# Moving 144 products of the first pass behind attention, spacing the conversions anew, and adding the second pass's results by transfer

## The chip, the cores and the metric

The kernel runs on one core of a Trainium2 chip. The metric is the device time of one execution in microseconds, the median of several runs. TensorE (PE in the profile), VectorE (DVE), ScalarE (ACT), GpSimd (POOL) and SyncE (SP) each work through a queue of their own; SP's and POOL's queues also start transfers. TensorE's clock has two levels, 1.2 and 2.4 GHz, and the profile gives the granted clock as a share of the higher.

## The reference

Attention with a block-causal mask feeds a bilinear feed-forward network, all in float32:

```python
scores = scale * q @ k^T                    # 8 batches, 8 heads, 576 x 576, head size 64
scores = where(block_i >= block_j, scores, -1e9)      # blocks of 64
attn = exp(scores - max) / (sum + 1e-9)
x = (attn @ v) as (4608 tokens, 512)
out = ((x @ w_a) * (x @ w_b)) @ w_out       # 512 -> 1536 -> 512
```

## The kernel before

**Products.** Every float32 product is done as three TensorE products of rounded high and low parts (high by high, high by low, low by high). So each operand is split: ACT rounds the high part (L110), and DVE or POOL subtracts it to get the low part (L113).

**Three passes over the feed-forward network.** Its 1536 inner columns are 12 blocks of 128, and each pass does four of them for all tokens.

The *first pass* (`first_pass`, L545) runs inside attention. Attention is laid out in 66 slots, one for each of 64 heads and two more, each with a softmax, transposes (L468) and products with v of different heads, in an order given by the table `SLOT` (L595). Between these pieces the loop issues as many of the first pass's products as `want(now)` (L583 to L588) says are due: 36 a slot from slot 18 on, where `now` counts slots. A product is 288 columns wide (L217); `ab_unit` (L228) multiplies x by w_a and w_b, DVE forms `hf` from the two (L243), ACT and POOL split it into `hh` and `hl`, and `o_unit` (L248) multiplies by w_out. The result goes to a buffer in DRAM, `part[0]`. Of 2304 products, 288 are left when attention ends, and 48 more (`tail`) close the pass. The halves of x that the pass reads lie in `xpool`, three sets (L536).

The *second and third pass* run after attention, the loop over `ps_`, six tiles of 2 x 384 tokens each. `pair_unit` (L701) does 42 products for each block and two half-tiles at once, by sums of weights and of x; DVE combines the PSUM results into `u` (L729 to L736), which is split into `h_z` by ACT and POOL. `upool` has two buffers of `u`. Then `pair_out` (L743) does eight outputs of 12 products each (L757). For each output `load_part` (L809) has loaded the partial sum from DRAM by SP, `out` (L814) adds it on DVE and stores the sum by SP: the second pass reads `part[0]` and writes `part[1]`, the third reads `part[1]` and writes the result. `sums_x` (L669) prepares x for the next tile on DVE, ACT and POOL.

**Conversions of weights.** The weights come as 64-bit words and DVE turns them into float32 in several steps (`convert`, L127 to L150, `sums`, L161 to L178), 68 steps for four blocks. `background` issues steps beside TensorE's products by a pace: one step for each `STEP` = 800 ns of products in what is left of the first pass, for the second pass's weights; one for each `STEP2` = 2800 ns in tiles 1 to 5 of the second pass, for the third pass's, which are stored to DRAM and loaded again. What is still missing at the end of a stage comes at once (`background(1e4)`, L854).

The order of instructions on each engine is made by a scheduler from the order in which the code issues them; within an engine's queue an instruction that waits holds up all behind it.

Of the kernel before, what the change touches and what calls it, by code (L numbers as in the profile page):

```python
# [9 lines left out]
F32 = mybir.dt.float32  # L10
F32R = mybir.dt.float32r
# [3 lines left out]
ALU = mybir.AluOpType  # L15
AX = mybir.AxisListType

P = 128
# [12 lines left out]
PQ = lambda nc: nc.sync  # L31
# [6 lines left out]
XFB = 2  # L38
MORE = 6
PREF = True  # L40
STEP = 800
STEP2 = 2800
LATE = 1
LO2 = lambda nc: nc.vector
CONVP = [1]*12
# [7 lines left out]
def attention_then_bilinear_ffn(  # L53
# [10 lines left out]
    nc = tc.nc  # L64
    B, H, D, S = kT.shape
    SQ = qT.shape[3]
    NF = wab.shape[0]
    DO, T = outT.shape
# [3 lines left out]
    NPAIR = H // 2  # L72
# [4 lines left out]
    HT = S // 2  # L77
# [4 lines left out]

    dram = ctx.enter_context(tc.tile_pool(name="dram", bufs=1, space=bass.MemoryType.DRAM))
    xd = dram.tile([DO, T], F32, name="xd")
    part = [dram.tile([DO, T], F32, name=f"part{i}") for i in range(2)]
    wabd = dram.tile([F2, KP, P, 2 * NW * P], F32, name="wabd")
    wod = dram.tile([F2, P, 2 * DO], F32, name="wod")

# [170 lines left out]
    xpool = pool(left, "xpool", 2)  # L259
# [39 lines left out]
    if WARM:  # L299
        z = apool.tile([P, NCH, W], F32R, tag="al", name="z")[:, 0]  # L300
        nc.vector.memset(f32(z), 0.0)
        ps = ps_mm.tile([P, 512], F32, tag="mm", name="warm")
# [181 lines left out]
    def values(i):  # L484

        b, h = divmod(i, H)
        n = f"{b}_{h}"
        t = heads.pop(i)
        ah, al = t["a"]
        hp = h // 2  # L490
        if h % 2 == 0:
            xs_all.setdefault(b, {})[hp] = xpool.tile([P, S], F32, tag="xf", name=f"xf{b}_{hp}", bufs=XFB)
        xf = xs_all[b][hp]
        av = ps_t.tile([P, W], F32, tag="av", name=f"av{n}")
        xo = xf[(h % 2) * D:(h % 2 + 1) * D]
        if i < NATIVE:
            an, vr = ah, t["vr"]
            av0 = ps_t.tile([P, 512], F32, tag="tp", name=f"av0{n}", bufs=2)
            nc.tensor.matmul(av0[:D, :BLK], vr[:, NCH], an[:, SIDE, SC[0]], start=True, stop=True)
            nc.scalar.copy(xo[:, :BLK], av0[:D, :BLK])  # L500

            at = [0] + [P * c - BLK for c in range(1, NCH)] + [W - BLK, W]
            for g in range(NCH + 1):
                cols = slice(at[g], at[g + 1])
                last = min(g, NCH - 1)
                for c in range(last + 1):
                    mark = nc.tensor.matmul(
                        av[:D, cols], vr[:, c], an[:, c, cols], start=(c == 0), stop=(c == last and g < NCH)
                    )
                if g == 2:  # L510
                    yield mark
            nc.tensor.matmul(av[:D, W - BLK:], vr[:, NCH], an[:, SIDE, SC[1]], start=False, stop=True)
            nc.scalar.copy(xo[:, BLK:], av[:D])
        else:
            v2 = t["v2"]
            for c in range(NCH):
                mark = nc.tensor.matmul(av[:, c0[c]:], v2[:, c], ah[:, c, c0[c]:], start=(c == 0), stop=False)  # L517
            yield mark
            av0 = ps_t.tile([P, 512], F32, tag="tp", name=f"av0{n}", bufs=2)
            for j, a in enumerate((ah, al)):  # L520
                nc.tensor.matmul(av0[:, :P], v2[:, NCH], a[:, SIDE, SIDE_T * P:][:, :P], start=(j == 0), stop=(j == 1))
            for c in range(NCH - 1, -1, -1):
                mark = nc.tensor.matmul(av[:, c0[c]:], v2[:, c], al[:, c, c0[c]:], start=False, stop=(c == 0))  # L523

            lo = apool.tile([D, S + BLK], F32, tag="avlo", name=f"avlo{n}", bufs=1)
            lo0, lo = lo[:, :P], lo[:, P:]
            nc.scalar.copy(lo0, av0[D:, :P])
            nc.vector.tensor_tensor(xo[:, :BLK], av0[:D, :BLK], lo0[:, :BLK], op=ALU.add)
            nc.vector.tensor_tensor(lo0[:, BLK:], av0[:D, BLK:P], lo0[:, BLK:], op=ALU.add)
            nc.scalar.copy(lo, av[D:])  # L530
            nc.vector.tensor_tensor(lo[:, W - BLK:], lo[:, W - BLK:], lo0[:, BLK:], op=ALU.add)
            nc.vector.tensor_tensor(xo[:, BLK:], av[:D], lo, op=ALU.add)
        if h % 2 == 1:
            xs = []
            for j in range(2):
                xh, xl = (xpool.tile([P, HT], F32R, tag=f"x{z}", name=f"x{z}{b}_{hp}_{j}", bufs=3 * NPAIR) for z in "hl")  # L536
                split(xh, xl, xf[:, j * HT:(j + 1) * HT], nc.scalar, nc.gpsimd)
                xs.append((xh, xl))
            XQ(nc).dma_start(xd[hp * P:(hp + 1) * P, b * S:(b + 1) * S], xf)
            xs_all[b][hp] = xs  # L540
        yield mark
# [3 lines left out]
    def first_pass():  # L545
        late = None
        for b in range(B):
            for j in range(2):
                ts = slice(b * S + j * HT, b * S + (j + 1) * HT)
                hs = {}  # L550

                def out(o, ps, ts=ts):
                    ob = h_tile(1, HT, F32, f"ob{ts.start}_{o}")
                    nc.scalar.copy(ob, ps)
                    PQ(nc).dma_start(part[0][o * P:(o + 1) * P, ts], ob)

                for f in range(F1):
                    xs = [xs_all[b][hp][j] for hp in range(NPAIR)]
                    yield from ab_unit(f, xs, HT, f"{b}_{j}_{f}", hs)
                    if f == 0 and late:  # L560
                        yield from late
                late = o_units(range(F1), hs, HT, f"{b}_{j}", out)
        tail.append(late)
# [9 lines left out]
    NH = B * H  # L573
    LAG = 2
# [8 lines left out]
    def want(now):  # L583

        n = (now - H - LAG) * per_slot - behind
        if now < 2 * H + LAG:
            n = (H * per_slot - behind) * (now - MOE_FROM) / (2 * H + LAG - MOE_FROM)
        return int(n)  # L588

    keep = None  # L590

# [7 lines left out]
    for s in range(NH + LAG):  # L599
# [11 lines left out]
        for g, m in steps:  # L611
# [17 lines left out]
            now = s + due / fill  # L629
# [154 lines left out]
    for _ in moe:  # L784
        k += 1
        background(min(k * HT / 2.4 / STEP, F2 * PER_F))
    left.close()
# [8 lines left out]
    for _ in tail[0]:  # L796
        k += 1
        background(min(k * HT / 2.4 / STEP, F2 * PER_F))
    start, pace = k * HT / 2.4 / STEP, STEP
    k = 0  # L800


    for ps_ in range(2):
        fs = list(range(F1 + ps_ * F2, F1 + (ps_ + 1) * F2))
        for tt in range(NT2):
            lastp = ps_ == 1 and tt == NT2 - 1
            pt = {}

            def load_part(j, o):  # L809
                ts = slice((2 * tt + j) * T2, (2 * tt + j + 1) * T2)  # L810
                pt[j, o] = ppool.tile([P, T2], F32, tag="pt", name=f"pt{j}_{o}_{tt}_{ps_}"), ts
                nc.sync.dma_start(pt[j, o][0], part[ps_][o * P:(o + 1) * P, ts])

            def out(j, o, ps):  # L814
                t, ts = pt[j, o]
                nc.vector.tensor_tensor(t, ps, t, op=ALU.add)
                nc.sync.dma_start((part[1] if ps_ == 0 else outT)[o * P:(o + 1) * P, ts], t)
                i = todo.index((j, o)) + 6
                if i < len(todo):
                    load_part(*todo[i])  # L820
# [76 lines left out]
```

## Time and profile before

| | us |
|---|---|
| median of 3 runs | 1269.23 |
| lowest, highest | 1268.36, 1271.0 |
| the profiled execution | 1273.54 |
| its span in the trace | 1271.6 |

| engine | busy us | share of the span |
|---|---|---|
| PE | 1235.8 | 97% |
| DVE | 1006.1 | 79% |
| ACT | 683.3 | 54% |
| POOL | 556.9 | 44% |

The span is what the trace holds, the time of the execution is 1.9 us more. Attention with the slots takes the first 637 us or so; what is left of the first pass follows, then the second pass from 697 us and the third from 983 us. The shares are means over these stages, which differ: in most of them TensorE is busy all the time, and what matters is where it isn't, or where a stage takes longer than its products.

### The profile page before, as it was taken

Reading aid. Unit: us, or ns where it says so; the run is one execution under the profiler, and the core shown is the slowest. Engines: PE = TensorE matmul, PEld = TensorE weight load, DVE = VectorE, ACT = ScalarE, POOL = GpSimd, SP = SyncE. Lnnn points to the kernel's source line nnn. Section 1 sums busy time; section 2 is a strip of 40 time slices with the busy share of each in tenths; the row PEclk is TensorE's granted clock in tenths of the full one; section 3 lists DMA queues with packets and bytes.
Section 4 is the critical chain, followed back from the end, with each engine's and each line's share of the span. In section 5 each row is a group of like instructions: output and inputs, shape, how many; then the busy total and the mean of one; then the engine's idle time right before and its main releaser. Section 6 shows DMA issues by size and latency. Waiting matters only on the chain.

```text
span 1271.6 us, 23516 instructions
## 1 busy us (share of the span) xinstructions
PE 1235.8 (97%) x7849; PEld 1172.4 (92%) x7849; DVE 1006.1 (79%) x2389; ACT 683.3 (54%) x1722; POOL 556.9 (44%) x679
## 2 busy tenths in 40 slices
PE   9988999999999999999998999999999999999998
PEld 5668999999999999999998999999999899999998
DVE  6979877777887777877799999899879877577553
ACT  5788787878887788777745423323313322122210
POOL 4667566556565565665423223222222223123231
PEclk8999999999999999999998999999999899999999
DMA  5557767777667767676225264364287752243131
GB/s 197 147 162 198 193 166 182 184 169 180 173 164 185 170 175 174 164 179 162 88 95 161 96 195 132 109 195 155 86 286 260 240 149 83 67 149 103 48 100 62
DMA packets 93496, 196.58 MB, mean 155 GB/s; under 512 B 11968, under 2 KB 52928, under 8 KB 93376
## 3 DMA queue, kind: packets, MB, share of 16 engines
q1 hardware_dynamic: 88768, 185.64, 51.8%
q10 hardware_dynamic: 4608, 9.44, 2.0%
q8 instruction: 63, 1.03, 0.3%
q14 instruction: 57, 0.47, 0.1%
HBM read 96.47 MB, written 47.19 MB: 113 GB/s over the span
## 4 chain that ended last, share of the span: by engine, by line
PE 74%; DVE 14%; issue 3%; DMA 3%; ACT 3%; POOL 2%; SPq 0%; ACTq 0%; DVEq 0%; POOLq 0%
PE pso_z L757 14%; PE ps L217 12%; PE tp L468 7%; PE psx_z L711 7%; PE psw_z L711 6%; PE pso L217 5%; PE psv_z L711 5%; PE s L392 4%; PE av L517 3%; PE psy_z L711 3%; PE av L523 3%; PE sl L392 2%; DMA kp<-kT 2%; DVE sw L147 1%; DVE nm L398 1%
## 5 line engine op out<-in xcount | busy, mean ns | idle before, releaser
L113 POOL TENSOR_TENSOR h_z<-u_z,h_z 128x384 fp32r<-128x384 f32 x96 | 111.0, 1157 | 395.4 <-ACT h_z L110 370.2
L217 PE MATMUL ps<-xh,wab 128*128 128x288 f32 x1024 | 241.4, 303 | 1.2 <-ACT a L241 1.2
L445 POOL TENSOR_SCALAR e<-e,rc 128x512 f32<-128x512 f32 (+3 forms) x256 | 153.1, 610 | 125.3 <-DVE rc L442 118.6
L757 PE MATMUL pso_z<-h_z,wo 128*128 128x384 f32 x1152 | 203.4, 335 | 1.2 <-POOL h_z L113 1.2
L757 PEld LDWEIGHTS pso_z<-h_z,wo 128*128 128x128 f32 x1152 | 199.7, 188 | 2.6 <-POOL h_z L113 2.6
L217 PEld LDWEIGHTS ps<-xh,wab 128*128 128x128 f32 x1024 | 171.9, 188 | 4.7 <-ACT a L241 1.4
L472 DVE TENSOR_TENSOR al<-tp,ah 128x512 fp32r<-128x512 f32 x224 | 131.5, 608 | 34.0 <-ACT ah L470 33.8
L217 PE MATMUL ps<-xl,wab 128*128 128x288 f32 x512 | 153.9, 301 | 0.0
L468 PE MATMUL tp<-ident,e 128*128 128x128 f32 x832 | 135.8, 278 | 11.1 <-POOL e L445 4.0
L470 ACT CAST ah<-tp 128x512 fp32r<-128x512 f32 x224 | 116.6, 533 | 50.8 <-PE tp L468 47.9
L110 ACT CAST h_z<-u_z 128x384 fp32r<-128x384 f32 x96 | 49.4, 514 | 164.4 <-DVE u_z L736 157.3
L217 PE MATMUL pso<-hh,wo 128*128 128x288 f32 x512 | 128.1, 311 | 4.4 <-ACT hh L110 4.4
L468 PEld LDWEIGHTS tp<-ident,e 128*128 128x128 f32 x832 | 100.4, 141 | 26.8 <-POOL e L445 10.4
L711 PE MATMUL psx_z<-xh,wab 128*128 128x384 f32 x384 | 118.2, 344 | 4.3 <-DVE u_z L729 3.6
L401 ACT ACTIVATE e<-s,nm 128x192 f32<-128x192 f32 (+2 forms) x192 | 101.7, 530 | 32.0 <-DVE nm L398 23.0
L711 PE MATMUL psw_z<-xh,wab 128*128 128x384 f32 x384 | 117.1, 341 | 1.3 <-DVE u_z L731 1.3
L711 PE MATMUL psv_z<-xh,wab 128*128 128x384 f32 x384 | 117.0, 339 | 0.0
L398 DVE TENSOR_REDUCE nm<-s 128x1 f32<-128x192 f32 (+3 forms) x256 | 109.9, 431 | 2.4
L217 PEld LDWEIGHTS ps<-xl,wab 128*128 128x128 f32 x512 | 96.4, 188 | 3.4
L217 PEld LDWEIGHTS pso<-hh,wo 128*128 128x128 f32 x512 | 88.4, 192 | 6.6 <-ACT hh L110 5.3
L113 POOL TENSOR_TENSOR v<-vr,v 128x320 fp32r<-128x320 f32 x56 | 50.4, 899 | 87.8 <-ACT v L110 71.3
L392 PE MATMUL s<-k,q 128*128 128x256 f32 x336 | 81.3, 322 | 3.1 <-ACT e L401 1.5
(142 smaller groups left out, 2926.3 us busy)
## 6 DMA issues: line engine op xcount, KB each, us to landing
k<-kp SPq DMA_DIRECT2D x112, 288.0 KB, 3.6
xr<-xd SPq DMA_DIRECT2D x48, 384.0 KB, 3.4
pt<-part SPq DMA_DIRECT2D x96, 192.0 KB, 3.5
q<-qp SPq DMA_DIRECT2D x112, 160.0 KB, 2.6
raww<-wab SPq DMA_DIRECT2D x24, 512.0 KB, 3.8
qp<-qT SPq DMA_DIRECT2D x32, 320.0 KB, 3.2
vr<-vm SPq DMA_DIRECT2D x64, 160.0 KB, 3.2
kp<-kT SPq DMA_DIRECT2D x32, 288.0 KB, 3.5
```

What stands on the lines that cost most here:

```text
L110: nc.scalar.copy(hi, src)
L113: return lo_eng.tensor_tensor(lo, src, f32(hi), op=ALU.subtract)
L217: mm = nc.tensor.matmul(ps, w_, d_, start=(i == 0), stop=(i == n - 1))
L392: mark = nc.tensor.matmul(ps[:, :w], qm[:, q0[t]:q0[t] + P], kk[:, :w], start=(i == 0), stop=(i == len(ks) - 1))
L398: nc.vector.tensor_reduce(nm[:, t:t + 1], view, axis=AX.X, op=ALU.max, negate=True)
L401: nc.scalar.activation(out, view, AF.Exp, bias=bias, accum_out=sm[:, t, :1])
L445: nc.gpsimd.tensor_scalar(ev, ev, rc[:, t:t + 1], 1.0, op0=ALU.mult, op1=ALU.mult)
L468: mark = nc.tensor.transpose(tp[:, c], src, ident)
L470: nc.scalar.copy(ah[:, :m, cols], tp[:, :m])
L472: return nc.vector.tensor_tensor(al[:, :m, cols], tp[:, :m], f32(ah[:, :m, cols]), op=ALU.subtract)
L711: nc.tensor.matmul(ps, wt[:, i, iw], j[:, ix], start=start and kp == 0 and i == 0 and j is xh, stop=kp == KP - 1 and i == 1, skip_group_ch ...
L757: nc.tensor.matmul(ps, wt[:, a, osl], b, start=i == 0, stop=i == 3 * len(fs) - 1)
```

## The change

It has three parts.

1. `DEFER` = 144: `want` is lowered evenly over the 48 slots from 18 on, so that 33 products a slot are due there instead of 36, and 432 products (with the tail 480) are left when attention ends, not 288 (336). x keeps four sets in `xpool`, not three.
2. `STEP` goes from 800 to 1050 and `STEP2` from 2800 to 1900.
3. One `part` in DRAM. In the second pass `out` copies the PSUM result by ACT and starts a transfer from POOL's queue that adds it to `part` in DRAM (`accum_op`); the load of the partial sum, DVE's addition and SP's store are left out. The third pass is as before, but reads `part`.

```diff
-STEP = 800
-STEP2 = 2800
+DEFER = 144
+STEP = 1050
+STEP2 = 1900
...
-    part = [dram.tile([DO, T], F32, name=f"part{i}") for i in range(2)]
+    part = dram.tile([DO, T], F32, name="part")
...
-  xh, xl = (xpool.tile([P, HT], F32R, ..., bufs=3 * NPAIR) for z in "hl")
+  xh, xl = (xpool.tile([P, HT], F32R, ..., bufs=4 * NPAIR) for z in "hl")
...
-        return int(n)
+        return int(n - DEFER * max(now - 2 * H - LAG, 0) / (NH - 2 * H))
...
-                nc.sync.dma_start(pt[j, o][0], part[ps_][o * P:(o + 1) * P, ts])
+                if ps_ == 1:
+                    nc.sync.dma_start(pt[j, o][0], part[o * P:(o + 1) * P, ts])
...
-                nc.vector.tensor_tensor(t, ps, t, op=ALU.add)
-                nc.sync.dma_start((part[1] if ps_ == 0 else outT)[o * P:(o + 1) * P, ts], t)
+                if ps_ == 0:
+                    nc.scalar.copy(t, ps)
+                    nc.gpsimd.dma_start(part[o * P:(o + 1) * P, ts], t, accum_op=ALU.add)
+                else:
+                    nc.vector.tensor_tensor(t, ps, t, op=ALU.add)
+                    nc.sync.dma_start(outT[o * P:(o + 1) * P, ts], t)
...
-    nc = bacc.Bacc("TRN2", target_bir_lowering=False, num_devices=1)
+    nc = bacc.Bacc("TRN2", ..., num_devices=1, dynamic_dma_scratch_size=4096)
```

Line numbers of the changed kernel are one higher up to L586 and two higher behind it. Whole programs differ so: DVE 2376 rows and 2328, ACT 1436 and 1484, POOL 684 and 732 (48 of them transfers), SP 681 and 587; TensorE's number is the same.

Three places show what moves. The first is DVE's queue in what is left of the first pass, behind attention; rows with L139 to L178 (after: L140 to L179) are steps of the conversions, and `hf` is what TensorE's next products need. Before:

```order
L243 TENSOR_TENSOR hf_0_1_10093<-ps_7_0_1_10071,a_0_1_10069 128x288
L178 TENSOR_TENSOR wab_9847<-mw_0_10017,wab_9847 128x512
L147 SCALAR_TENSOR_TENSOR sw_1_10086<-raww_1_10014,sw_1_10086 128x512
L143 TENSOR_SCALAR mw_1_10087<-raww_1_10014 128x512
L145 SCALAR_TENSOR_TENSOR mw_1_10087<-raww_1_10014,mw_1_10087 128x512
L243 TENSOR_TENSOR hf_0_2_10137<-ps_7_0_2_10116,a_0_2_10114 128x288
L149 TENSOR_TENSOR xw_1_10088<-mw_1_10087,sw_1_10086 128x512
L172 TENSOR_TENSOR mw_1_10087<-xw_1_10088 128x128 x2
L172 TENSOR_TENSOR mw_1_10087<-mw_1_10087,xw_1_10088 128x128
L139 TENSOR_SCALAR sw_0_10165<-raww_0_10084 128x512
L172 TENSOR_TENSOR mw_1_10087<-xw_1_10088,mw_1_10087 128x128
L177 TENSOR_TENSOR wab_9847<-xw_1_10088,wab_9847 128x384
```

After, on the same queue:

```order
L244 TENSOR_TENSOR hf_1_2_9917<-ps_6_1_2_9897,a_1_2_9895 128x288
L140 TENSOR_SCALAR sw_1_9945<-raww_1_9849 128x512
L179 TENSOR_TENSOR wab_9649<-mw_0_9852,wab_9649 128x512
L144 TENSOR_SCALAR mw_1_9946<-raww_1_9849 128x512
L244 TENSOR_TENSOR hf_1_3_9961<-ps_6_1_3_9940,a_1_3_9938 128x288
L146 SCALAR_TENSOR_TENSOR mw_1_9946<-raww_1_9849,mw_1_9946 128x512
L148 SCALAR_TENSOR_TENSOR sw_1_9945<-raww_1_9849,sw_1_9945 128x512
L244 TENSOR_TENSOR hf_0_0_9997<-ps_7_0_0_9983,a_0_0_9981 128x288
```

Two or three steps stand between two `hf` where four to seven stood.

The second place is DVE's queue at the first unit of the third pass (`u_z_0_8`), whose four PSUM results TensorE can only go on with once `u` has read them. Before:

```order
L816 TENSOR_TENSOR pt_3_5_0_13308<-pso_3_z_5_13385,pt_3_5_0_13308 128x384
L143 TENSOR_SCALAR mw_2_13418<-raww_2_13400 128x512
L147 SCALAR_TENSOR_TENSOR sw_2_13417<-raww_2_13400,sw_2_13417 128x512
L145 SCALAR_TENSOR_TENSOR mw_2_13418<-raww_2_13400,mw_2_13418 128x512
L676 TENSOR_TENSOR xr_1_13531<-xr_1_13531 128x384
L149 TENSOR_TENSOR xw_2_13419<-mw_2_13418,sw_2_13417 128x512
L729 TENSOR_TENSOR u_z_0_8_13498<-psx_z_0_8_13467,u_z_0_8_13498 128x384
L139 TENSOR_SCALAR sw_2_13432<-raww_2_13415 128x512
L143 TENSOR_SCALAR mw_2_13433<-raww_2_13415 128x512
L731 TENSOR_TENSOR u_z_0_8_13499<-psw_z_0_8_13468,u_z_0_8_13498 128x384
```

After:

```order
L684 TENSOR_TENSOR xt_1_0_13633<-xr_1_13484,xt_1_0_13633 128x384
L677 TENSOR_TENSOR xt_1_1_13713<-xr_1_13488,xr_1_13486 128x384
L678 TENSOR_TENSOR xr_1_13486<-xr_1_13486 128x384
L681 TENSOR_TENSOR xt_1_1_13713<-xr_1_13488,xr_1_13486 128x384
L684 TENSOR_TENSOR xt_1_1_13713<-xr_1_13488,xt_1_1_13713 128x384
L731 TENSOR_TENSOR u_z_0_8_13449<-psx_z_0_8_13418,u_z_0_8_13449 128x384
L733 TENSOR_TENSOR u_z_0_8_13450<-psw_z_0_8_13419,u_z_0_8_13449 128x384
```

No conversion and no addition of `pt` stands there any longer; the rows ahead of `u` prepare x.

The third place is POOL's queue at the end of a tile of the second pass: `xl` is the next tile's x, `h_z_1_4` the split of the next tile's first unit. Before:

```order
L113 TENSOR_TENSOR h_z_0_7_0_10868<-u_z_0_7_10872,h_z_0_7_0_10867 128x384
L691 TENSOR_TENSOR xl_1_1_10919<-xr_1_10673,xh_1_1_10909 128x768
L692 TENSOR_TENSOR xl_1_1_10919<-xt_1_1_10910,xh_1_1_10909 128x384
L113 TENSOR_TENSOR h_z_1_4_1_11089<-u_z_1_4_11091,h_z_1_4_1_11088 128x384
L113 TENSOR_TENSOR h_z_1_4_0_11087<-u_z_1_4_11090,h_z_1_4_0_11086 128x384
```

After:

```order
L694 TENSOR_TENSOR xl_1_1_10912<-xt_1_1_10903,xh_1_1_10902 128x384
L821 DMA part<-pt_0_0_0_10751 128x384
L821 DMA part<-pt_1_0_0_10752 128x384
L821 DMA part<-pt_2_0_0_10753 128x384
L821 DMA part<-pt_3_0_0_10754 128x384
L821 DMA part<-pt_0_0_0_10755 128x384
L821 DMA part<-pt_1_0_0_10756 128x384
L821 DMA part<-pt_2_0_0_10942 128x384
L821 DMA part<-pt_3_0_0_10948 128x384
L114 TENSOR_TENSOR h_z_1_4_1_11081<-u_z_1_4_11083,h_z_1_4_1_11080 128x384
```

The tile's eight transfers stand between the two.

## Rows read from the trace of the kernel before

**Rows 1.** Windows by stage; the header names the columns, (x) counts instructions.

```profile
core 0: us, PE busy (x) PEld busy (x) DVE busy (x) ACT busy (x) POOL busy (x), PEclk, DMA share, GB/s
637.50:697.00 59.50, 52.37 (x366) 50.45 (x365) 57.64 (x114) 29.73 (x64) 15.06 (x13) 0.94 0.40 127
697.00:745.30 48.30, 47.32 (x266) 45.77 (x265) 47.89 (x81) 19.69 (x33) 15.58 (x12) 1.00 0.42 136
...
887.10:934.60 47.50, 47.16 (x266) 45.98 (x266) 40.57 (x65) 12.09 (x22) 13.26 (x10) 1.00 0.44 140
934.60:983.30 48.70, 47.09 (x265) 46.13 (x264) 40.13 (x66) 13.11 (x23) 13.24 (x10) 1.00 0.78 276
983.30:1035.80 52.50, 49.51 (x266) 48.71 (x265) 46.36 (x80) 19.03 (x31) 13.77 (x10) 0.93 0.67 219
1035.80:1082.30 46.50, 46.50 (x266) 46.33 (x266) 31.38 (x51) 11.38 (x20) 13.18 (x10) 1.00 0.35 104
```

**Rows 2.** Chain of waits in stage A: start, length, the work.

```profile
674.26 9.60 PE ps L217 x72
```

**Rows 3.** TensorE's waits, 637.5 to 746: total, times, longest, in us.

```profile
PE pso L217 <- ACT hh L110: 4.4, 4, 1.6
PE pso L217 <- POOL hl L113: 2.7, 4, 0.9
```

**Rows 4.** DVE's groups in stage A: count, busy us, mean ns, idle before.

```profile
L147 DVE SCALAR_TENSOR_TENSOR sw<-raww,sw 128x512 int32<-128x512 int32 x8 | 6.1, 763 | 0.0
...
L243 DVE TENSOR_TENSOR hf<-ps,a 128x288 f32<-128x288 f32 x10 | 4.5, 449 | 0.0
```

**Rows 5.** Windows of two stretches at a lower clock, columns as in Rows 1.

```profile
687.80:694.70 6.90, 4.81 (x19) 4.36 (x19) 6.87 (x14) 5.80 (x10) 1.66 (x2) 0.51 0.81 254
991.60:998.50 6.90, 6.12 (x19) 6.12 (x20) 6.31 (x13) 3.02 (x5) 0.34 (x1) 0.51 0.91 302
```

**Rows 6.** Timeline, third pass's start: start, length, engine, work, [idle before <-releaser].

```profile
989.82 0.44 PE L711 MATMUL psx_z<-xh,wab 128*128 128x384 f32 x1 [1.73 <-DVE u_z L729]
992.38 0.69 PE L711 MATMUL psw_z<-xh,wab 128*128 128x384 f32 x1 [1.25 <-DVE u_z L731]
...
989.21 0.55 DVE L729 TENSOR_TENSOR u_z<-psx_z,u_z 128x384 f32<-128x384 f32 x1
991.10 0.43 DVE L139 TENSOR_SCALAR sw<-raww 128x512 int32<-128x512 int32 x1 [1.34 <-DMA raww<-wo]
```

**Rows 7.** Windows of slots, L217 alone: length, PE, PEld, clock, DMA, GB/s.

```profile
135.47:174.53 39.06, 24.23 (x126) 18.93 (x124) 1.00 0.72 187
303.38:322.76 19.38, 13.28 (x74) 10.76 (x72) 1.00 0.76 194
175.00:626.00 451.00, 305.24 (x1656) 247.23 (x1656) 1.00 0.67 167
```

**Rows 8.** ACT's cast of `kp`, 175 to 626, and what ended its waits.

```profile
L344 ACT CAST kp<-kp x22: 672/674/696, 179.1 to 585.9; 128x576 fp32r<-128x576 f32 x22
...
  DMA q<-qp: 4.6, 3
  DMA kp<-kT: 1.3, 3
```

**Rows 9.** DVE's addition of `pt` in one tile, columns as in Rows 4.

```profile
L816 DVE TENSOR_TENSOR pt<-pso_z,pt 128x384 f32<-128x384 f32 x9 | 4.8, 547 | 0.0
```

**Rows 10.** Timelines of POOL, DVE and ACT around a tile's end.

```profile
779.43 2.58 POOL L691 TENSOR_TENSOR xl<-xr,xh 128x768 fp32r<-128x768 f32 x1
781.97 1.74 POOL L692 TENSOR_TENSOR xl<-xt,xh 128x384 fp32r<-128x384 f32 x1
...
800.83 1.03 POOL L113 TENSOR_TENSOR h_z<-u_z,h_z 128x384 fp32r<-128x384 f32 x1 [17.13 <-ACT h_z L110]
...
801.13 1.01 DVE L139 TENSOR_SCALAR sw<-raww 128x512 int32<-128x512 int32 x1
...
809.04 0.48 ACT L728 COPY u_z<-psy_z 128x384 f32<-128x384 f32 x1 [0.48 <-PE psy_z L711]
```

More of the change, by code (lines that the diff above doesn't have):

```diff
@@ L535, in values @@
             for j in range(2):
-                xh, xl = (xpool.tile([P, HT], F32R, tag=f"x{z}", name=f"x{z}{b}_{hp}_{j}", bufs=3 * NPAIR) for z in "hl")
+                xh, xl = (xpool.tile([P, HT], F32R, tag=f"x{z}", name=f"x{z}{b}_{hp}_{j}", bufs=4 * NPAIR) for z in "hl")
                 split(xh, xl, xf[:, j * HT:(j + 1) * HT], nc.scalar, nc.gpsimd)
@@ L554, in out @@
                     nc.scalar.copy(ob, ps)
-                    PQ(nc).dma_start(part[0][o * P:(o + 1) * P, ts], ob)
+                    PQ(nc).dma_start(part[o * P:(o + 1) * P, ts], ob)
                 for f in range(F1):
@@ L886 @@
     }
-    nc = bacc.Bacc("TRN2", target_bir_lowering=False, num_devices=1)
+    nc = bacc.Bacc("TRN2", target_bir_lowering=False, num_devices=1, dynamic_dma_scratch_size=4096)
     args = [
```

## The prediction

> **What bounds the kernel now.** I read the windows by stage first. TensorE is busy nearly everywhere, so the question is where a stage is longer than its products need. A product of 288 columns costs 9.60 us / 72 = 133 ns where nothing disturbs it [rows 2], and a tile of the second and third pass takes 46.5 us at its best, with PE busy for the whole of it [rows 1]. Against these two prices the stages after attention stand so. The stretch from 637.5 to 697.0, which I call stage A (the left-over products of the first pass), holds 366 products: 366 x 0.1333 = 48.8 us, but lasts 59.5, so 10.7 us over. The second pass's six tiles begin at 697.0; the first is 1.8 us over, the four from 745.3 to 934.6 together 189.3 - 186.0 = 3.3, the sixth 2.2. The third pass's first tile (983.3 to 1035.8) is 6.0 over [rows 1]. So two places are to be had: A and that last tile.
>
> In A the reader should look at DVE's column: 57.64 of 59.50 us busy [rows 1]. TensorE waits there for `hh` and `hl`, ACT's and POOL's halves of `hf`, 7.1 us up to 746 [rows 3]. `hf` is a short DVE operation (449 ns) that stands in a queue of conversions (763 ns for one of their kinds) [rows 4]. Behind the wait the clock falls: 0.51 granted, the 1.2 GHz level, for 6.9 us, and again for 6.9 us in the third pass's first tile [rows 5]. At half speed 6.9 us do the work of 3.5, so each costs about 3.4 us and is part of the 10.7 and the 6.0. The second place has the same cause: TensorE waits 1.73 and 1.25 us for `u_z`, two DVE operations of 0.55 us which run among conversions, one of which itself waited for its load [rows 6].
>
> In the slots TensorE is the bound too: 46 slots of 36 products take 451.0 us, 9.80 each, and an undisturbed pair 19.38, 9.69 each [rows 7].
>
> **The change, part by part.**
>
> *Fewer products in the slots.* 48 slots lose 3 products each: 144 x 0.1333 = 19.2 us, if TensorE stays the bound. It is uncertain that it does. The nearest rows are four early slots with about 31 products: 39.06 / 4 = 9.77 us, where a clean slot of 31 takes 9.69 - 5 x 0.1333 = 9.03. They lose 0.74 a slot, the slots of 36 only 9.80 - 9.69 = 0.11 [rows 7]. On a straight line, 33 products would lose 0.49, 0.38 more than now, 48 x 0.38 = 18 us, and the whole gain here would be gone. Against the line: those four still lie in the start-up, and slots of 36 are clean for dozens in a row. One thing does not shrink with PE's work: ACT's `kp` cast, once per two slots, waited for a load in 6 of 22 cases, 5.9 us [rows 8], and POOL and the pair's other work follow it. Every two slots become 0.8 us shorter (6 x 0.1333); if about half of that, 0.43, is lost in the six late pairs and in some eight others partly, that is some 4.3 us. With 0.7 for the edge from POOL's scaling to the transposes I take 5 us of give-back, nearer to the slots of 36 (33 is nearer to 36 than to 31); ends: -2 and +18. Term: -19.2 + 5 = -14.2.
>
> *The same products after attention, conversions further apart.* A then has 366 + 144 = 510 products, 68.0 us for TensorE. DVE's work there is its 57.64 plus six more `hf` (6 x 0.449 = 2.7): 60.3 us, now 8 under TensorE's where it was 9 over (57.6 against 48.8). So A turns from DVE-bound to PE-bound. What stays is that the last `hh` and `hl` have no products behind them to hide in: the longest waits, 1.6 + 0.9 [rows 3], and 0.5 elsewhere; 3 us over. The stretch at the lower clock goes with the long wait. A becomes 71 us: +11.5 against 59.5. Ends for what is left over: 0 and 7. The order shows conversions further apart between two `hf`, and the seven steps that no longer fit come with the first pair unit, where four PSUM banks of products stand ready; I take 0, with 1.5 either way.
>
> *Conversions of the third pass, faster.* 168 products of 160 ns in a tile are 26.9 us of the planner's time; at 2800 that is 9.6 steps, 48 in five tiles of the 68, and 20 come in one lump at the pass's end. At 1900 it is 14.1, 70.7 in five, so no lump is left. The first `u_z` of the third pass then find DVE free, as in the next tile (46.50 us) [rows 1]. I keep 0.4 over: -5.6. Ends: -6 and -2.
> The price lies in tiles 1 to 5 of the second pass: 4.5 more steps a tile at about 0.85 us is +3.9 of DVE, and the eight additions of `pt` go, 8 x 0.547 = 4.4 [rows 9]. DVE stays at about 40.6 of 47.5 [rows 1], so 0; ends -2 and +5.
>
> *Results added by the transfer.* In each tile of the second pass 8 loads on SP, 8 additions and 8 stores go; 8 ACT copies and 8 transfers issued by POOL come. ACT has the room: 12 of 47.5 us busy [rows 1], about 0.5 a copy [rows 10]. PSUM banks come free at the copy rather than at an addition that also waits for a load; no cost. POOL's issue is shown nowhere. Its place is: after `xl` (the last ends at 783.7, 8 us into a tile's output products), before the next tile's `h_z` (800.83) [rows 10]. `u` has two buffers, so the next tile's third unit needs the first unit's split to be over before its ACT copy at 809.04 [rows 10]. From 783.7 to there less two splits of 1.0 to 1.4 is 22 to 23 us, and TensorE has some 2 more before it misses `u`: 8 issues fit up to about 3.1 us each. Below that it costs nothing; above, 8 x (d - 3.1) a tile, six tiles. For d the nearest rows are POOL's own operations on a 128x384 tile, 1.03 to 1.74, and as a high bound its longest there, 2.58 [rows 10]. I take 1.2: 0 us. DRAM has room: 140 GB/s moved in such a tile, 276 where the weights load [rows 1].
> Here the slowest case hangs on DVE and POOL holding each other up: the conversion `L139` takes 1.01 us beside POOL's split and 0.43 alone [rows 6, 10]. The Trainium skill (page "SBUF — State Buffer", section "SBUF: two separate sides") says that GpSimd writes the descriptors of such transfers itself and is shut out while certain DVE operations run; a later section gives 620 ns alone and 3100 ns beside a DVE copy. The pair of 1.01 and 0.43 agrees that the two block each other; no run here shows it for transfers. By that figure eight issues would take 24.8 us, right at the limit, and the sum would hardly change.
>
> **The sum.** -14.2 (slots) + 11.5 (A) - 5.6 (third pass) = -8.3 us. The profiled execution took 1273.54, 4.3 above the median of 1269.23, which I take for something outside these terms; so 1265.2 for it and 1269.2 - 8.3 = 1261 for the median.
>
> **The rivals.** About 0.2% (2.5 us) is what a measurement of this kernel can tell from no change: faster is below 1266.7, slower above 1271.8.
> 1. *Slots at the early rate.* Attention's chain, not TensorE, sets the slot at 33 products. Price +18 in place of +5: 1261 + 13 = 1274, slower. It decides from 16 us of give-back (0.33 a slot). For it: the four slots of 31. Against: clean slots of 36, and the early place of the four. 0.13.
> 2. *DVE still binds A.* The conversions still stand ahead of `hf`, each later product waits as now, and A keeps its 10.7: 1261 + 7.7 = 1269, same. For it: still 60 of 71 us busy. Against: PE's queue has 144 products to take meanwhile. 0.12.
> 3. *POOL is held.* d = 4 gives 8 x 0.9 x 6 = 43 us: 1304, slower. Decides from d = 3.3, where 8 x 0.2 x 6 = 10 eats the gain. For it: DVE is 85% busy beside it. 0.06.
> 4. *The lump only spreads.* The 20 steps in the second pass's tiles make TensorE wait there, 5 us: 1266. 0.10.
> My forecast 0.59.
>
> **How the numbers follow.** Faster: 0.59 + 0.08 of rival 4 + 0.01 = 0.68. Same: rival 2 and the rest of 4, 0.14. Slower: rivals 1 and 3 with little less, 0.18. The forecast's own ends: best -2 slots, 0 over in A, -6: about 1251; worst with 10 of give-back and 5 in the tiles, 1271. The range 1252 to 1271 leaves out rivals 1 and 3 and a little below.
>
> **What would show it.** Right: slots about 9.5 us each on the mean (9.80 - 0.40 + 0.10); A about 71 us with DVE well under it; the third pass's first tile at 47 and full clock; POOL's `part` transfers over by the next tile's second unit; second-pass tiles at 47. Wrong: slots at 9.75 or more (rival 1); `hf` waits in A as long as before (2); `h_z` late for TensorE at a tile's second half (3); pass tiles at 48 (4). If A gains but the slots don't, the products were merely carried from one cover to no cover.

## The result and the profile after

The changed kernel takes 1274.67 us (median of 8 runs, 1274.07 to 1279.55), the kernel before 1270.12 in the same comparison (8 runs, 1263.68 to 1273.62): a ratio of 1.0042, 95% interval 1.0023 to 1.0061. It is 0.4% slower. The forecast was 1261 us, faster.

The two profiled executions, 1273.54 before and 1274.54 after, differ by 1.0 us only. That of before was 3.4 above its median, that of after at its median. Stage by stage (attention's end is the end of its last TensorE product; a tile runs from its first product to the next tile's):

| stage, us | before | after | difference | forecast |
|---|---|---|---|---|
| attention and slots, to the end of attention | 637.5 | 630.5 | -7.0 | -14.2 |
| rest of the first pass (A) | 59.5 | 68.4 | +8.9 | +11.5 |
| second pass, tile 0 | 48.3 | 48.9 | +0.6 | 0 |
| second pass, tiles 1 to 4 | 189.2 | 194.7 | +5.4 | 0 |
| second pass, tile 5 | 48.75 | 47.8 | -0.95 | 0 |
| third pass, tile 0 | 52.5 | 46.5 | -6.0 | -5.6 |
| the rest | 235.8 | 236.0 | +0.1 | 0 |

The windows of the changed kernel by stage answer to [rows 1], with the same columns: A, two tiles of the second pass, its last, the third pass's first.

```profile
core 0: us, PE busy (x) PEld busy (x) DVE busy (x) ACT busy (x) POOL busy (x), PEclk, DMA share, GB/s
630.50:698.90 68.40, 67.35 (x508) 67.02 (x507) 59.61 (x121) 35.69 (x77) 18.83 (x18) 1.00 0.33 105
747.70:796.30 48.60, 47.20 (x267) 45.79 (x266) 42.35 (x72) 20.15 (x38) 21.19 (x19) 1.00 0.50 128
796.30:845.10 48.80, 47.20 (x266) 45.88 (x265) 41.32 (x67) 19.89 (x38) 20.26 (x19) 1.00 0.54 145
942.40:990.20 47.80, 47.17 (x265) 45.91 (x265) 40.05 (x58) 18.64 (x34) 19.16 (x17) 1.00 0.81 244
990.20:1036.70 46.50, 46.50 (x266) 46.33 (x266) 31.61 (x51) 11.85 (x21) 15.33 (x13) 1.00 0.53 154
```

In A TensorE is busy 67.35 of 68.40 us, DVE 59.61, and the clock is at its full share, 1.00, where it was 0.94: the turn from DVE-bound to TensorE-bound came as forecast. The third pass's first tile is clean. The loss lies in two places: the slots, which give back more than forecast, and tiles 1 to 4 of the second pass, which should have cost nothing.

**The slots.** The 44 slots from 18 to 61 show it best. I take 9.69 us for a slot with 36 products, as in [rows 7], and three products less, 9.29, with 33; what the 44 slots take above that (426.4 and 408.8 us) I call the loss. It is 5.7 us before and 17.7 after. These are the windows of the 44 slots before and after, with L217 (after: L218) alone, and the columns length, PE, PEld, clock, DMA, GB/s:

```profile
174.50:606.60 432.10, 291.84 (x1586) 236.46 (x1584) 1.00 0.69 173
173.50:600.10 426.60, 276.87 (x1454) 220.15 (x1452) 1.00 0.68 173
```

Two slots alone, 24 and 36, last 13.4 and 13.2 us (9.9 and 9.8 before). What stands in slot 24, from the timelines of SP (issues), ACT, POOL and TensorE of the changed kernel:

```profile
223.83 0.60 SPq L359 DMA_DIRECT2D q<-qp  x1
...
227.89 0.34 SPq L323 DMA_DIRECT2D qp<-qT  x1
...
229.29 0.45 SPq L322 DMA_DIRECT2D kp<-kT  x1
...
231.32 0.74 ACT L338 ACTIVATE qp<-qp 128x640 fp32r<-128x640 f32 x1 [2.33 <-issue]
...
235.91 0.67 ACT L345 CAST kp<-kp 128x576 fp32r<-128x576 f32 x1 [0.88 <-DMA kp<-kT]
...
236.65 1.42 POOL L346 TENSOR_TENSOR kp<-kp 128x576 f32<-128x576 f32 x1 [2.65 <-ACT kp L345]
238.05 1.88 POOL L446 TENSOR_SCALAR e<-e,rc 128x512 f32<-128x512 f32 x2
...
236.99 0.56 PE L393 MATMUL s<-k,q 128*128 128x320 f32 x2 [0.76 <-ACT e_s L402]
...
239.37 0.33 PE L469 MATMUL tp<-ident,e 128*128 128x128 f32 x1 [1.28 <-POOL e L446]
```

`qp` and `kp`, the inputs for a pair of heads, have one buffer each. The next pair's load can only start when the last copy out of the buffer (`q<-qp`, issued at 223.83) has landed; it is issued at 227.89. ACT then sits before `qp` for 2.33 us and again before `kp`, with the exponentials of the running slot queued behind. POOL's half of `kp` waits for ACT's and stands ahead of POOL's scaling of `e`. TensorE waits for both, the exponentials and the scaled `e`. In the 6 us of those copies the transfers had nothing to spare either: the DMA share is 0.98.

```profile
222.00:228.00 6.00, 5.89 (x43) 5.50 (x42) 4.93 (x18) 4.79 (x16) 3.37 (x6) 1.00 0.98 218
```

**The second pass.** In the changed kernel all of TensorE's waits there are for DVE's `u`, 7.7 us in 14 waits, nearly all of them at a unit's first `u`. That line for the second pass (total, times, longest), before and after:

```profile
PE psx_z L711 <- DVE u_z L729: 1.9, 5, 1.2
PE psx_z L713 <- DVE u_z L731: 7.3, 13, 1.2
```

One of these waits, in the timelines of TensorE and DVE in tile 1:

```profile
760.34 0.44 PE L713 MATMUL psx_z<-xh,wab 128*128 128x384 f32 x1 [0.78 <-DVE u_z L731]
...
756.43 1.28 DVE L150 TENSOR_TENSOR xw<-mw,sw 128x512 f32<-128x512 f32 x1
757.75 1.20 DVE L173 TENSOR_TENSOR mw<-xw 128x128 f32<-128x128 f32 x2
758.87 0.28 DVE L173 TENSOR_TENSOR mw<-mw,xw 128x128 f32<-128x128 f32 x1
759.07 0.55 DVE L178 TENSOR_TENSOR st<-xw,st 128x384 fp32r<-128x384 f32 x1
759.54 0.28 DVE L173 TENSOR_TENSOR mw<-xw,mw 128x128 f32<-128x128 f32 x1
759.74 0.55 DVE L731 TENSOR_TENSOR u_z<-psx_z,u_z 128x384 f32<-128x384 f32 x1
```

Six operations of a conversion, 3.3 us, stand between a unit's end and the next unit's first `u`, and two rows of them are long while POOL splits `h_z` (the step that took 1.28 us here took 0.68 at 768.25, with POOL at rest). The units and the outputs of one tile, apart, show where DVE's time went. Tile 2 of the kernel before, then of the changed one, units first:

```profile
792.32:822.90 30.58, 30.36 (x169) 29.22 (x169) 26.15 (x47) 8.73 (x17) 6.41 (x6) 1.00 0.41 147
822.90:839.55 16.65, 16.65 (x98) 16.65 (x97) 16.62 (x23) 5.82 (x10) 6.57 (x4) 1.00 0.58 166
```

```profile
796.28:828.43 32.15, 30.55 (x169) 29.23 (x169) 27.30 (x51) 10.40 (x21) 8.96 (x9) 1.00 0.43 118
828.43:845.08 16.65, 16.65 (x98) 16.65 (x98) 14.02 (x17) 9.49 (x18) 11.28 (x10) 1.00 0.75 197
```

The outputs take 16.65 us in both. DVE got 2.6 us freer there (16.62 to 14.02), where TensorE never waited for it, and 1.2 us fuller in the units, where it does: 30.58 became 32.15.

POOL's transfers stayed short; whether they have a part in it at all the runs below tell. The view of their line: minimum, median and maximum length of an issue in ns, and the time to landing.

```profile
L821 POOL DMA_DIRECT2D part<-pt x48: 851/1164/1677, 739.0 to 991.4; - x48
...
DMA to landing us min/median/max: 3.7/5.7/11.5
```

### The profile page after: what moved, and what is told of

It reads as the page before. It is cut to its first block, busy times and chain, and to the rows that moved or that the text cites. A ratio compares the mean times of both kernels' runs of the same rounds, so it can differ in the third digit from the quotient of the medians.

```text
span 1272.6 us, 23454 instructions
## 1 busy us (share of the span) xinstructions
PE 1233.5 (97%) x7849; PEld 1167.9 (92%) x7849; DVE 995.3 (78%) x2341; ACT 701.8 (55%) x1770; POOL 600.3 (47%) x727
## 4 chain that ended last, share of the span: by engine, by line
PE 71%; DVE 14%; ACT 4%; issue 3%; DMA 3%; POOL 2%; SPq 1%; ACTq 0%; DVEq 0%; POOLq 0%
PE pso_z L759 16%; PE ps L218 11%; PE tp L469 6%; PE psw_z L713 6%; PE psx_z L713 6%; PE pso L218 5%; PE psv_z L713 5%; PE s L393 3%; PE psy_z L713 3%; PE av L524 2%; DVE nm L399 2%; PE av L518 2%; PE sl L393 2%; DMA q<-qp 1%; POOL e L446 1%
## 5 line engine op out<-in xcount | busy, mean ns | idle before, releaser
L218 PE MATMUL ps<-xh,wab 128*128 128x288 f32 x1024 | 249.4, 305 | 1.2 <-ACT a L242 1.2
L446 POOL TENSOR_SCALAR e<-e,rc 128x512 f32<-128x512 f32 (+3 forms) x256 | 163.2, 649 | 113.2 <-DVE rc L443 102.7
L218 PEld LDWEIGHTS ps<-xh,wab 128*128 128x128 f32 x1024 | 173.2, 188 | 5.2 <-ACT a L242 1.4
L218 PE MATMUL ps<-xl,wab 128*128 128x288 f32 x512 | 152.2, 297 | 0.0
L218 PE MATMUL pso<-hh,wo 128*128 128x288 f32 x512 | 126.0, 307 | 0.5 <-ACT a L242 0.3
L218 PEld LDWEIGHTS ps<-xl,wab 128*128 128x128 f32 x512 | 96.5, 188 | 2.6
L114 POOL TENSOR_TENSOR hl<-hf,hh 128x288 fp32r<-128x288 f32 x64 | 54.7, 854 | 83.2 <-ACT hh L111 83.2
L218 PEld LDWEIGHTS pso<-hh,wo 128*128 128x128 f32 x512 | 87.5, 189 | 2.7 <-ACT a L242 0.5
```

The costliest lines, as they stand in the source:

```text
L114: return lo_eng.tensor_tensor(lo, src, f32(hi), op=ALU.subtract)
L218: mm = nc.tensor.matmul(ps, w_, d_, start=(i == 0), stop=(i == n - 1))
L446: nc.gpsimd.tensor_scalar(ev, ev, rc[:, t:t + 1], 1.0, op0=ALU.mult, op1=ALU.mult)
```

## The experiments

Two theories came out of the two traces. *The slots*: a pair's inputs go round a loop through one buffer, its length does not shrink with the products, and shorter slots run into it. *The second pass*: conversions are issued beside the units' products only, so the denser pace fills the very stretch in which TensorE waits for DVE. The rivals: POOL's queue or the softmax sets the slots; ACT's copies and POOL's transfers lengthen the tiles. The stages of all runs are measured as in the table above, and the loss in slots 18 to 61 against the same nominal times (9.49 for 34.5 products). Each run has one trace.

### Each part alone

The first part alone, with the `STEP` that goes with it, put into the kernel before:

```diff
+DEFER = 144
-STEP = 800
+STEP = 1050
...
-    bufs=3 * NPAIR
+    bufs=4 * NPAIR
...
+        return int(n - DEFER * max(now - 2 * H - LAG, 0) / (NH - 2 * H))
...
+    nc = bacc.Bacc(..., dynamic_dma_scratch_size=4096)
```

> Before with the first part alone: DEFER 144, four sets of x, STEP 1050 (and the smaller scratch for transfers, without which four sets do not fit). Theory 'the slots give most of it back': attention ends 6 to 9 us earlier than before (637 us), not 14; what is left of the first pass then takes 68 to 69 us instead of 60; the second and third pass keep their times (286 and 288): 1270 to 1274 in all. Rival 'the slots lost time for another reason, not for their fewer products' (the third part's or the other paces' doing): attention ends at 622 to 625, 1264 to 1267 in all.

Measured: 1271.53 us, ratio 0.9997 (0.9979 to 1.0015), no difference. Attention ends at 632.0, the loss in the slots is 19.9 us (slots 24 and 36: 4.8 and 4.2), A takes 68.4. So the slots give most of their time back with this part alone: they win 5.5 us, and A becomes 8.9 longer.

```profile
632.00:700.40 68.40, 67.35 (x508) 67.01 (x508) 59.62 (x121) 35.72 (x77) 18.85 (x18) 1.00 0.37 119
```

The second pace alone:

```diff
-STEP2 = 2800
+STEP2 = 1900
```

> Before with STEP2 1900 alone. Theory 'denser conversions lengthen the second pass': its tiles 1 to 4 go from 47.3 to 48.5 or more each, since first additions of u wait behind more conversion steps, while the third pass's first tile falls from 52.5 to 46.5: 1268 to 1271 in all, nothing won. Rival 'ACT's copies and POOL's transfers lengthen the tiles': tiles stay at 47.3, third pass's first tile 46.5, and 1263 to 1265 in all.

Measured: 1277.45 us, ratio 1.0047 (1.0031 to 1.0064), slower than the kernel before and than either expectation. Tiles 1 to 4 take 48.6, 49.7, 48.7 and 48.7; the third pass's first tile 49.9. Two of these tiles and the third pass's first in windows:

```profile
743.80:792.40 48.60, 47.18 (x266) 45.78 (x265) 45.01 (x78) 16.07 (x29) 13.44 (x10) 1.00 0.49 154
792.40:842.10 49.70, 47.33 (x266) 45.66 (x265) 46.07 (x78) 16.29 (x28) 12.94 (x10) 1.00 0.52 183
987.30:1037.10 49.80, 46.19 (x265) 45.68 (x264) 35.49 (x59) 13.34 (x23) 13.15 (x10) 1.00 0.48 159
```

The tiles grow as in the changed kernel with neither ACT's copies nor POOL's transfers in them, which settles that question. The third pass's first tile did not fall to 46.5, as both expectations had it. What holds it shows in one wait of SP's queue (985.5 to 988.6; total, times, longest) and the timelines of SP, DVE and TensorE:

```profile
SPq L817 <- DVE pt L816: 1.9, 1, 1.9
...
988.06 0.32 SPq L817 DMA_DIRECT2D part<-pt  x1
988.49 0.37 SPq L665 DMA_DIRECT2D xr<-xd  x1
...
992.41 0.56 DVE L675 TENSOR_TENSOR xt<-xr,xr 128x384 f32<-128x384 f32 x1 [2.38 <-DMA xr<-xd]
...
995.27 0.44 PE L711 MATMUL psx_z<-xh,wab 128*128 128x384 f32 x1 [3.61 <-DVE u_z L729]
```

A store of a sum waits for DVE's addition, and the last load of the next x stands behind that store: it is issued 1.2 us after the third pass's first product (987.26), where in the changed kernel it is issued 5.6 us or more ahead of it (by 984.64; the pass starts at 990.20). DVE waits for that x ahead of `u`, and TensorE for `u`. So the lump of conversions was not all that stood in this tile.

The second and third pass add up to 2.9 us over those of before (577.5 against 574.6), less than the 7 of the medians; the profiled execution was at 1274.76, 2.7 below its median. What differs between executions of this kernel one trace doesn't show.

The third part alone (the second pass's results copied by ACT and added by POOL's transfer, as in the diff of the change; pace 2800):

> Before with the third part alone: ACT copies and POOL's adding transfers in the second pass, STEP2 at 2800. Theory 'denser conversions lengthen the second pass': tiles 1 to 4 stay at 47.0 to 47.4, the third pass's first tile stays at 50 to 52.5 because the lump of 20 steps is still there: 1268 to 1271. Rival 'copies and transfers lengthen the tiles': tiles 1 to 4 at 48.5, 1274 to 1276 in all.

Measured: 1272.79 us, ratio 1.0019 (1.0000 to 1.0038): at the edge of no difference, a little above the first expectation and below the rival's. Tiles 1 to 4 take 47.0, 47.0, 47.5, 47.5, as before, and the third pass's first tile 52.9.

```profile
742.40:789.40 47.00, 46.73 (x265) 45.85 (x265) 38.42 (x60) 17.19 (x33) 20.16 (x18) 1.00 0.47 109
789.40:836.40 47.00, 46.68 (x266) 45.96 (x265) 37.79 (x59) 16.59 (x32) 19.45 (x17) 1.00 0.49 126
980.10:1033.00 52.90, 48.20 (x265) 47.06 (x265) 41.72 (x72) 17.21 (x30) 20.83 (x15) 0.97 0.63 196
```

DVE has 3.2 and 5.0 us more room in these two tiles (41.7 and 42.8 us busy before), about half of it in the outputs, and TensorE gains nothing by it in either half: what counts is not how full DVE is, but what stands in its queue just ahead of `u`.

The changed kernel without its first part:

```diff
-DEFER = 144
-STEP = 1050
+DEFER = 0
+STEP = 800
```

> The changed kernel without its first part (DEFER 0, STEP 800; four sets of x stay). Theory 'the slots give most of it back': attention ends at 635 to 638 as before, the rest of the first pass takes 60, the second pass 291, the third 282: 1268 to 1271, some 4 below the changed kernel. Rival 'the first part is worth what was forecast (-2.7) and the loss lies behind it': 1276 or more, above the changed kernel.

Measured: 1271.84 us, ratio 1.0009 (0.9988 to 1.0031). Attention ends at 638.0 with 7.1 us lost in the slots, A takes 59.3, the second pass 290.8, the third 282.4. Behind attention the other two parts give one thing for the other: +4.5 in the second pass, -5.9 in the third. The time is 2.8 us below the changed kernel's, with intervals that overlap, so it rules out the rival but does not price the first part; between the two traces that part wins 7.5 us in the slots and loses 9.1 in A.

### The two mechanisms

Two buffers for a pair's `qp` and `kp`; the room comes from fewer x tiles:

```diff
-    qp = apool.tile([P, 2, SQ], F32, tag="qp", ..., bufs=1)
-    kp = apool.tile([P, 2, S], F32, tag="kp", ..., bufs=1)
+    qp = apool.tile([P, 2, SQ], F32, tag="qp", ..., bufs=2)
+    kp = apool.tile([P, 2, S], F32, tag="kp", ..., bufs=2)
...
-    bufs=4 * NPAIR
+    bufs=13
```

> The changed kernel with two buffers for a pair's qp and kp in place of one (13 sets' worth of x tiles instead of 16 make the room). Theory 'a pair's loads wait for the pair before in the one buffer, and this loop does not shrink with the products': the slots 24, 36 and 50 fall to about 9.5 us, of the 18 to 20 us lost in slots 18 to 62 some 5 are left, attention ends at 618 to 622: 1261 to 1266. Rival 'POOL's scaling of e, or the engines' load, sets the slots': attention ends at 629 to 632 as in the changed kernel, 1273 to 1276.

And, to see that it isn't the x tiles, `bufs=13` alone:

> The changed kernel with 13 x tiles a kind instead of 16, and nothing else: what the room for the pair's buffers was taken from. Theory: no change, attention ends at 629 to 632 and the loss in slots 18 to 62 is 17 to 20: 1273 to 1276. Rival 'it was the number of x tiles that helped the slots': attention ends at 618 to 622, 1261 to 1266.

Measured: with the two buffers 1264.36 us, 0.9947 (0.9929 to 0.9966); with 13 x tiles alone 1276.85, 1.0053 (1.0035 to 1.0071), like the changed kernel. Attention ends at 619.2 against 630.4, and the loss in the slots is 9.9 against 17.0. The slots 24 and 36 last 9.8 and 10.4 us. TensorE's waits in the slots (total, times, longest), first with 13 x tiles alone, then with the pair's two buffers:

```profile
PE tp L469 <- POOL e L446: 7.2, 10, 1.5
PE s L393 <- ACT e L402: 2.5, 2, 1.8
```

```profile
PE tp L469 <- POOL e L446: 4.3, 10, 1.3
PE tp L469 <- DVE s L414: 1.6, 4, 0.6
```

The waits for ACT, which sat before the pair's loads, are gone. The loop is shown: two buffers take 7 us out of slots 18 to 61, and 4 us out of the slots ahead of them. Expected were 5 us of loss left; 9.9 are. TensorE's waits for POOL's scaled `e` stay at 4.3 us in ten waits, where the kernel before had one of 1.4 us: here is a second cause, which the buffers do not take away.

The third pass's conversions issued beside the outputs too, in the changed kernel:

```diff
-STEP2 = 1900
+STEP2 = 3200
...
             def out(j, o, ps):
+                nonlocal k
                 t, ts = pt[j, o]
                 if ps_ == 0:
+                    k += 3 * F2
+                    background(start + k * T2 / 2.4 / pace)
```

> The changed kernel with the third pass's conversions issued beside the output products too, not beside the units' alone (STEP2 3200, counted over both; same 68 steps, no lump). Theory 'too many steps stand among the units, none in the outputs, where the additions had been': tiles 1 to 4 of the second pass go from 48.5-48.8 back to 46.8 to 47.3, the third pass's first tile stays at 46.5: 6 us less than the changed kernel, 1268 to 1270. Rival 'the tile lacks DVE time as a whole, or ACT's copies delay u': tiles stay at 48.5, 1274 to 1276.

Measured: 1267.13 us, ratio 0.9986 (0.9970 to 1.0003), no difference from the kernel before and 7.5 us below the changed kernel. Tiles 1 to 4 take 46.7, 46.7, 47.2, 47.3, the third pass's first 46.5. The units and outputs of tile 1:

```profile
747.50:777.50 30.00, 29.96 (x170) 29.46 (x169) 23.68 (x42) 8.31 (x18) 9.32 (x9) 1.00 0.40 113
777.50:794.10 16.60, 16.60 (x97) 16.60 (x96) 16.57 (x25) 9.51 (x18) 11.26 (x9) 1.00 0.67 160
```

The same 68 steps, ACT's copies and POOL's transfers still there: DVE is full in the outputs (16.57 of 16.60), has room in the units, and these take 30.00 us (31.9 in the changed kernel, 30.3 before). That the steps fit beside the outputs because the additions are off DVE is likely, since DVE is full there without them; but no run issues the steps there with the additions still on DVE.

### Half the deferral, and everything together

The changed kernel with 72 products moved, 34 or 35 in a slot (`DEFER = 72`, `STEP = 925`):

> The changed kernel with half the deferral (72 products, 34 or 35 a slot, STEP 925). If the loss comes on evenly with the products taken away: 11 to 13 us lost in slots 18 to 62 (4 to 7 at 36, 18 to 20 at 33), attention ends at 633 to 635. If there is a point from which the pair's loop binds, below 34.5: 5 to 8 lost, attention ends at 627 to 630. The rest of the first pass 60 to 61, since DVE and TensorE need about the same there.

Measured: 1266.13 us, ratio 0.9967 (0.9951 to 0.9983): with half the products moved the change is 0.3% faster than the kernel before. Attention ends at 627.9, the loss in slots 18 to 61 is 6.2 us, A takes 61.6. So the loss does not come on evenly: 3.8 to 7.1 in four traces at 36 products, 6.2 at 34.5, 17.0 to 19.9 in four traces at 33. Between 34.5 and 33 there is a point from which the loop binds.

All of it with three amounts of deferral (two buffers for `qp` and `kp`, conversions beside the outputs too):

> All of it without the deferral: DEFER 0, three sets of x, two buffers for qp and kp, conversions beside the outputs too. If both theories hold: slots of 36 lose about 1 us instead of 4 to 7 (attention ends at 631 to 633), the rest of the first pass 59.5 to 60.5, second pass 282 to 284, third 282.4: 1258 to 1262. If the pair's buffers have no part: attention ends at 635 to 638, 1262 to 1266.

> All of it with the deferral: DEFER 144, two buffers for qp and kp, conversions beside the outputs too. If both theories hold: attention ends at 618 to 622, the rest of the first pass 68 to 69, second pass 283 to 286, third 282.4: 1254 to 1260, below the one without the deferral, since TensorE then sets both the slots and what follows. If the pair's buffers have no part: attention ends at 629 to 632, 1266 to 1270, above the one without the deferral.

> The kernel with everything and half the deferral (72, STEP 925). If the slots lose less at 34.5 products than at 33 (POOL's queue): 4 to 6 lost, attention ends at 622 to 625, the rest of the first pass 60 to 62, 1251 to 1255, below both the one with 144 and the one with none. If the loss is even: 1256 to 1258.

| products moved | time | ratio, interval | loss in slots 18 to 61 | attention's end | A |
|---|---|---|---|---|---|
| 0 | 1256.74 | 0.9898 (0.9878 to 0.9918) | 3.6 | 630.2 | 59.4 |
| 72 | 1254.62 | 0.9881 (0.9857 to 0.9905) | 6.1 | 622.7 | 61.7 |
| 144 | 1257.43 | 0.9902 (0.9883 to 0.9920) | 9.9 | 618.7 | 69.0 |

All three beat the kernel before by 1.0 to 1.2%, and the changed kernel's median by 1.4 to 1.6%. Among themselves they agree within their intervals, so the order of the three, which two of the expectations had forecast, isn't shown by the times; by the traces the half amount has the least of both stages together (684.4 us, against 689.6 and 687.7).

With two buffers the loss comes on evenly, 3.6, 6.1 and 9.9 us, where with one it jumped. So the slots' loss has two parts. From 36 to 33 products it grows by 12.0 us with one buffer and by 6.3 with two: about half of the growth is the loop, and the other half stays, most of it in the waits for POOL's scaled `e` (none with 36 products and two buffers, 4.8 us with 33). At 36 the slots lose 3.6 us with two buffers, where about 1 was expected.

The A of the half amount:

```profile
622.70:684.40 61.70, 58.78 (x436) 57.63 (x435) 56.64 (x115) 31.56 (x70) 14.98 (x14) 1.00 0.42 135
```

TensorE has 58.78 of 61.70 us, DVE 56.64: the 72 products fill what DVE's conversions left empty, and the next 72 make the stretch 7.3 us longer and win 4.0 in the slots.

With 144 moved and the pair's loop out of the way, 9.9 us are still lost, half of it in waits for POOL's scaled `e`. POOL's queue has the splits of x ahead of it in every second slot, so I moved these to DVE in the kernel with everything and 144:

```diff
-  split(xh, xl, xf[:, j * HT:(j + 1) * HT], nc.scalar, nc.gpsimd)
+  split(xh, xl, xf[:, j * HT:(j + 1) * HT], nc.scalar, nc.vector)
```

> The kernel with everything and the deferral, and with x's low parts (xl, two of 0.8 us in every second slot) subtracted by DVE instead of POOL. Theory 'what is left to lose in the shorter slots is POOL's queue, in which xl, hl and kp stand ahead of the scaling of e': TensorE's waits for e fall from 4.8 us to under 2.5, the loss in slots 18 to 62 from 9.7 to some 5, attention ends at 613 to 616: 1252 to 1255. Rival 'the softmax's own length sets it': attention ends at 618 to 620, 1257 to 1259.

Measured: 1276.77 us, ratio 1.0044 (1.0024 to 1.0063); 27.0 us lost in the slots. TensorE's waits there:

```profile
PE tp L469 <- DVE al L473: 9.9, 10, 1.6
PE tp L469 <- POOL e L446: 5.2, 11, 1.5
```

Neither theory had this. The waits for `e` are no shorter with POOL relieved, and new ones for `al`, DVE's low halves of the transposes, come on top. It speaks against the splits of x as the cause; but DVE also makes `rc`, which the scaling needs, so the run doesn't tell POOL's queue from the softmax's own length. That rest, some 5 us, stays open.

## Why the prediction was wrong, point by point

From forecast to result there are 12.8 us (-8.3 forecast, +4.5 measured between medians): slots 7.1, tiles 5.0, A -2.6, the third pass -0.3, and 3.4 for the profiled execution.

**The slots: the step "I take 5 us of give-back".** The give-back was 19.2 - 7.0 = 12.2 us. The mechanism named there was at work, ACT held by `kp`'s load [rows 8], but it was priced by half a slot's shortening a pair, some tenths each. Where the slack of a loop is used up, the loss comes in lumps: two slots of about 4 us each, four more over 1. The loop itself was not seen, though of the 5.9 us of waits in [rows 8] 4.6 are put down to `q<-qp`, the copy out of the buffer; `qp` goes round it ahead of `kp`. And "0.7 for the edge from POOL's scaling to the transposes" was too small: TensorE's waits for the scaled `e` went from 1.4 us to 6.2, and 4.3 were left when the loop was out of the way. The choice between the ends rested on "33 is nearer to 36 than to 31"; it is the other way round, three products from 36 and two from 31, and distance was the wrong measure besides: the half deferral shows the loss hardly grown at 34.5, so the rise lies between there and 33. Rival 1 had the size more nearly (+18), with the early slots as its row [rows 7].

**The second pass: the step "+3.9 of DVE, and the eight additions go, 4.4 ... so 0".** The second pass became 5.0 us longer. Both figures were near: over tiles 1 to 4, DVE's busy time a tile rose by 2.9 us with the pace alone and fell by 3.8 with the third part alone, and with both DVE's total fell a little (in tile 2 41.3 us after, 42.8 before). The sum was made over the tile, while most of the additions had stood in the outputs and the conversions stand in the units, ahead of `u`. TensorE waits for `u` alone, and each of the four tiles became 1.1 to 1.6 us longer. This is rival 4 in effect, at its price of 5 us; 0.10 was too little for it, since the code says where `background` is called. The third part alone (additions off DVE, nothing won) and the steps issued beside the outputs (all of it back) show from both sides that the place of the steps counts, not their sum.

**A: right, and better than said.** 68.4 us for 68.0 of products; the 3 us for the last `hh` and `hl` did not come. (The 144 products bring four `hf`, not six; DVE's 59.61 us for 60.3 hardly show it.) Rival 2 is out.

**The third pass: right.** -6.0 for -5.6. The first `u` found DVE free, as in the order, and the stretch at the lower clock [rows 5] is gone. With the pace alone only 2.6 us of it came, and in that trace a load of x stood late behind a store of a sum. The third part takes these stores away and so has its use here; one trace of each kernel shows it.

**POOL's issue: right.** 1.16 us in the median for the 1.2 taken, at most 1.68; rival 3's limit was never near. The Trainium skill (page "SBUF — State Buffer", section "A bandwidth-pool intuition that's wrong (but worth ruling out)") gives 620 ns for such a transfer alone and 3100 ns beside a DVE copy. That is the time of a transfer, and the prediction set it against POOL's time for an issue. Here the transfers landed 3.7 to 11.5 us after their issue, and DVE ran no copy beside them, so no run here shows what the page states.

**The median: the step "4.3 above the median, which I take for something outside these terms".** In the comparison with the changed kernel it was 3.4. The slots with 36 products, alike in code (one kernel keeps four sets of x), ended at 637.5, 636.0, 634.5 and 638.0 us in four traces, with 4 to 7 us of loss. So the slots vary from trace to trace, and the prediction took its rows from one trace with later slots than two of the others and started from the median all the same. Whether that makes up the 3.4 us isn't shown: there is no second trace of the kernel before.

**The range.** 1252 to 1271 left rival 1 out at 0.13. Its upper end took the tiles' 5 us, but only 10 us of give-back, where the slots' own end was 18. With that end it would have reached 1261 + 13 + 5 = 1279.

## What to carry to other kernels

When work is moved off a busy engine in one stretch and put on it in another, make the sum for each stretch in which someone waits for that engine, not for the tile: the additions taken off DVE paid for nothing in the units, and issuing the same steps beside the outputs too gave back all of it. Before taking work out of a loop that TensorE fills, look for the other loops that go round with it, above all single buffers refilled by a transfer, and count their slack in their slowest turns: they cost nothing until the point where they cost all at once. Where two stages trade work, look for the amount that just fills the idle engine of the second; here the traces point to about 72 of 144 products, while the times do not tell the three amounts apart.

## What the runs showed of the hardware

An addition by transfer of a 128x384 tile from POOL's queue took 0.85 to 1.68 us of POOL and landed after 5.7 us in the median (3.7 to 11.5), where the plain store from SP's queue had landed after some 3 us. No compute engine waited for it here; SP's queue did, 8.2 us in four waits, before the third pass's first loads of the sums, and the tile there took its 46.5 us all the same. In the units DVE's work is longer beside POOL's: the same conversion step took 1.28 us beside POOL's split and 0.68 without, and the two short steps behind it 1.20 and 0.48. By these figures an estimated 1.3 of the 3.3 us that stood ahead of `u` came from that.
